# Hash-bucketed attention with a maxout layer behind it: one burst of eight heads in five chunks, 29 weight tiles, VectorE's third addition from the second batch on

## The chip, the cores and the metric

The kernel runs on one core of a Trainium2 chip. Its engines work side by side, each through its own list of instructions in order: TensorE (PE, matmuls; its weight loads are shown as PEld), VectorE (DVE), ScalarE (ACT), GpSimd (POOL) and SyncE (SP, which here only issues DMAs). They wait for each other by semaphores. SBUF is the memory on the chip that all engines work from, PSUM is what matmuls write into. The metric is the device time of one execution in microseconds, lower is better.

## The reference

Four batches, eight heads, 768 positions, 64 dimensions per head. Every query and key gets a bucket number of six bits, the signs of its six projections; a query attends only to keys of its own bucket. The heads' outputs side by side are the input of a layer whose hidden value is the largest of three products.

```python
q_bits = (np.einsum('bhsd,dk->bhsk', q, proj) > 0)        # the same for k
mask = q_bucket[:, :, :, None] == k_bucket[:, :, None, :]
scores = np.where(mask, scale * np.matmul(q, k.transpose(0, 1, 3, 2)), -1e9)
scores = scores - np.max(scores, axis=-1, keepdims=True)
attn = np.exp(scores)
attn = attn / (np.sum(attn, axis=-1, keepdims=True) + 1e-09)
x = np.matmul(attn, v)          # heads laid side by side: 3072 x 512
h = np.maximum(np.maximum(x @ w1, x @ w2), x @ w3)        # 3072 x 768
out = h @ w_out                                           # 3072 x 512
```

## The kernel before

**Chunks and units.** The queries of the first batch are cut into three chunks of 256 (chunks 0 to 2), those of each other batch into two of 384 (chunks 3 to 8). The bits are appended to queries and keys as further rows of the contraction, so that one matmul gives score and mask together. A *unit* is one matmul group of scores, 768 columns wide in all (for a 384-wide chunk: two key blocks of 128), and one exponential on ScalarE, which writes the unnormalised weights into one of `NAT = 24` weight tiles `AT` (`scores`, L298 and L306). A chunk of 384 has 24 units, three per head; there are 192 units, 48 per batch.

**The main loop** at the end of the kernel takes one step `u` per unit, and the order in which it issues instructions is the order on every engine: the scores of unit `u + 1`; whatever the lists `at` hold for this step; one feed-forward group (from the second batch on 1.15 per step, by a credit); a hash, if one is due; the bursts that are due (`todo`).

**A burst** (`burst`) turns the weights of four heads of a chunk into normalised attention. `sums` adds the weights over the keys by matmuls with a matrix of ones (L358), four heads side by side in four groups of 32 output columns. VectorE then transposes the sums (L365), adds a small number, takes the reciprocal and spreads it by a second transpose into `rb` (L369). `values` multiplies the weights with the value vectors, twice 24 matmuls (L380), and VectorE adds the sum of the values and multiplies with `rb` while it moves the result from PSUM into `xT` (L387). Then the weight tiles are free again. The burst of heads 0 to 3 of chunks 3 to 7 stands twelve steps ahead of that of heads 4 to 7, each four steps behind the last unit that it needs (`LAG`): steps 63 and 75 for chunk 3, 87 and 99 for chunk 4, 111 and 123 for chunk 5, 135 and 147 for chunk 6, 159 and 171 for chunk 7.

**Additions.** From chunk 3 on VectorE adds the three weight tiles of a head (`add`, L329, two instructions, each two steps behind its unit), so that the sums need two key blocks in place of six. From chunk `THIRD_ADD = 5` on a third, half as wide addition (L332) folds the two blocks into one.

**The feed-forward layer** of a chunk (`ffn_groups`) is put in line two steps behind its last burst and is worked off in the steps that follow, so that in steps 55 to 93 (units of chunks 3 and 4) the groups of the 256-wide chunks 1 and 2 are worked off. A group is four matmuls (L413) into one PSUM bank; of three groups the first is copied (by VectorE at L420 for 256-wide chunks, by ScalarE at L418 for 384-wide ones), the other two are taken into a running maximum by VectorE (L422). Final products (L457) come last in each chunk; ScalarE copies them out. Sums, values, hashes and groups share four PSUM banks, which are taken in the order in which they were given back (`bank`, `give`). The scores have two double banks of their own.

**Preparing heads.** From the second batch on queries and keys are loaded in sets of four heads (`load_quad`; sets 4 to 7 on GpSimd's queue), transposed by VectorE (`turn`, L202, four instructions a set and side), narrowed to bf16 by GpSimd (`narrow`, L207) and copied into place by DMAs on SyncE's queue (`place`). `quad_hash` makes the bits (L221, then one VectorE instruction, then four DMAs on SyncE's queue one step later) and is the last reader of the transposed tiles `t32`. `SPREAD` gives the steps of the transposes of sets 4 and 5 (from step 61) and 6 and 7 (from step 100).

Of the kernel before, what the change touches and what calls it, by code (L numbers as in the profile page):

```python
# [9 lines left out]
FP32 = mybir.dt.float32  # L10
FP16 = mybir.dt.float16
BF16 = mybir.dt.bfloat16
AluOp = mybir.AluOpType
# [4 lines left out]
def kernel(  # L18
# [12 lines left out]
    nc = tc.nc  # L31
    B, H, S, D = q.shape
    NBITS = proj.shape[1]
    P = 128
    NM = S // P
    HALF = S // 2
# [4 lines left out]
    Q = 32  # L41
# [8 lines left out]
    RS = 2.0 ** -5  # L50
    SCALE = 0.125 / (RS * RS)
    EPS = 2.0 ** -60
    NAT = 24
    SPREAD = {2: (61, 9), 3: (100, 12)}
    THIRD_ADD = 5
    LAG = (1, 4)
    ATW = 776

    konst = ctx.enter_context(tc.tile_pool(name="konst", bufs=1))
    nat_pool = ctx.enter_context(tc.tile_pool(name="nat", bufs=6))  # L60
    t32_pool = ctx.enter_context(tc.tile_pool(name="t32", bufs=3))
    t16_pool = ctx.enter_context(tc.tile_pool(name="t16", bufs=3))
    s_pool = ctx.enter_context(tc.tile_pool(name="spool", bufs=6))
    b_pool = ctx.enter_context(tc.tile_pool(name="bpool", bufs=2))
    vo_pool = ctx.enter_context(tc.tile_pool(name="vopool", bufs=4))
    small = ctx.enter_context(tc.tile_pool(name="small", bufs=4))
    ad_pool = ctx.enter_context(tc.tile_pool(name="adpool", bufs=5))
    ys_pool = ctx.enter_context(tc.tile_pool(name="yspool", bufs=2))
    rb_pool = ctx.enter_context(tc.tile_pool(name="rbpool", bufs=2))
    x_pool = ctx.enter_context(tc.tile_pool(name="xpool", bufs=3))  # L70
# [7 lines left out]
    pj2 = konst.tile([P, Q], FP32, name="pj2")  # L78
    pst = konst.tile([Q, 2, NBITS], FP32, name="pst")
    ones = konst.tile([P, Q], FP16, name="ones")  # L80
    at_tiles = [konst.tile([P, ATW], FP16, name=f"AT{i}", tag=f"AT{i}") for i in range(NAT)]
    warm = h_pool.tile([P, HALF], FP16, tag="ht", name="warm")
    w_sb = [konst.tile([P, NJC, DF], FP16, name=f"w{i}_sb", tag=f"w{i}_sb") for i in range(3)]
# [6 lines left out]
    def bank():  # L90
        i = free_banks.pop(0)
        return i, bank_tiles[i]

    def give(i):
        if i is not None:
            free_banks.append(i)


    nat, t32, t16, s_of, where, v_at = {}, {}, {}, {}, {}, {}
# [143 lines left out]
    def load_weights(i):  # L243
        if i == 3:
# [8 lines left out]
    chunks = [(b, w * n, w) for b in range(B) for w in (THIRD if b == 0 else HALF,)  # L253
              for n in range(S // w)]
    NCH = len(chunks)

    def parts_of(c):
        return chunks[c][2] * NM // (2 * HALF)
# [10 lines left out]

    at_free = list(range(NAT))  # L270
    at_form = [THIRD] * NAT
    at_of = {}
# [6 lines left out]
    def block_of(b, m):  # L279
        return 2 * (m % MH) + m // MH if b == 0 else m  # L280
# [29 lines left out]
    def weights_of(c, h, m):  # L310
        w = chunks[c][2]
        nb = 2 * HALF // w
        return blocks(at_tiles[at_of[unit_at[c, h, m // nb]]], w)[:, m % nb, :]
# [8 lines left out]
    def add(c, h, n):  # L322
# [6 lines left out]
        nc.vector.tensor_tensor(out=sum_of[c, h][:], in0=t[0], in1=t[n], op=AluOp.add)  # L329
        if n == 2 and c >= THIRD_ADD:  # L330
            t = sum_of[c, h]
            nc.vector.tensor_tensor(out=t[:, 0, :], in0=t[:, 0, :], in1=t[:, 1, :], op=AluOp.add)  # L332

    def sum_blocks(c, h):
        w = chunks[c][2]
        if (c, h) in sum_of:
            t = sum_of[c, h]
            return [t[:, j, 0:w] for j in range(1 if c >= THIRD_ADD else 2)]
        return [weights_of(c, h, m)[:, 0:w] for m in range(NM)]

    def burst(c, i):
        b, q0, w = chunks[c]
        held = {}
        rb = []

        def own_bank(key):
            if c == NCH - 1 and i == 1 and key != 1:
                return None, sc_ps.tile([P, 2, 512], FP32, tag="sc", name="sc")[:, 0, :]
            return bank()

        def sums(m0, m1):
            if m0 == 0:
                held["s"] = own_bank("s")
            sm = held["s"][1]
            bs = [sum_blocks(c, 4 * i + x) for x in range(4)]
            for m in range(len(bs[0])):
                for x in range(4):
                    nc.tensor.matmul(sm[Q * x : Q * (x + 1), 0:w], ones[:, :], bs[x][m],  # L358
                                     start=(m == 0), stop=(m == len(bs[0]) - 1))
            if m1 == NM:  # L360
                ys = ys_pool.tile([P, HALF], FP32, tag="ys", name="ys")
                rr = small.tile([P, HALF // Q], FP32, tag="rr", name="rr")
                n = w // Q
                rb.append(rb_pool.tile([P, HALF], FP32, tag="rb", name="rb"))
                nc.vector.transpose(ys[:, 0:w], sm[:, 0:w])  # L365
                give(held["s"][0])
                nc.vector.tensor_scalar(out=rr[:, 0:n], in0=ys[:, 0:w:Q], scalar1=EPS * S, scalar2=None, op0=AluOp.add)
                nc.vector.reciprocal(rr[:, 0:n], rr[:, 0:n])
                nc.vector.transpose(rb[0][:, 0:w], rr[:, 0:n].unsqueeze(2).to_broadcast((P, n, Q)))  # L369

        def values(side, m0, m1):
            if m0 == 0:
                held[side] = own_bank(side)
            av = held[side][1]
            first = (b, i, side) not in sv_of
            n = w + 1 if first else w
            for m in range(m0, m1):
                cb = block_of(b, m)
                for x in range(4):
                    nc.tensor.matmul(av[Q * x : Q * (x + 1), 0:n], v_at[2 * b + i][:, x, cb * D + side : (cb + 1) * D : 2],  # L380
                                     weights_of(c, 4 * i + x, m)[:, 0:n], start=(m == 0), stop=(m == NM - 1))
            if m1 == NM:
                if first:
                    sv_of[b, i, side] = small.tile([P, 1], FP32, tag=f"sv{side}", name="sv")
                    nc.vector.tensor_scalar(out=sv_of[b, i, side][:], in0=av[:, w : w + 1], scalar1=EPS, scalar2=None,
                                            op0=AluOp.mult)
                nc.vector.scalar_tensor_tensor(out=xt_of(c)[:, 2 * i + side, 0:w], in0=av[:, 0:w],  # L387
                                               scalar=sv_of[b, i, side][:], in1=rb[0][:, 0:w], op0=AluOp.add, op1=AluOp.mult)
                give(held[side][0])
                if side == 1:  # L390
                    for h in range(4 * i, 4 * i + 4):
                        for n in range(parts_of(c)):
                            a = at_of[unit_at[c, h, n]]
                            if b == 0 and i == 1:
                                nc.gpsimd.memset(blocks(at_tiles[a], HALF)[:, :, HALF : HALF + 2], 1.0)
                                at_form[a] = HALF
                            at_free.append(a)

        return sums, values


    def ffn_groups(c):
# [79 lines left out]
    with tc.manual_schedule():  # L482
# [10 lines left out]
        load_quad(1, 2, range(4), nc.sync)  # L493
        nc.vector.memset(pj2[:], 0.0)
        nc.vector.memset(ones[:], 1.0)
        for t in at_tiles:
            nc.vector.memset(blocks(t, THIRD)[:, :, THIRD : THIRD + 2], 1.0)
        for hd in range(2):
# [75 lines left out]
        hash_at = {}  # L574
        for g in range(2, NQUAD):
            b2, i2 = divmod(g, 2)
            need = UPB * b2 + 12 * i2
            for n, side in enumerate((1, 0)):
                name = (side, g)
                if g > 3:  # L580
                    us = [SPREAD[b2][0] + SPREAD[b2][1] * (8 * i2 + 4 * n + n2) // 4 for n2 in range(4)]
                    for x in range(4):
                        when(us[0] - 14 + x, load_quad, side, g, (x,), nc.gpsimd)
                else:
                    us = [need - {2: 26, 3: 23}[g] + 4 * n + n2 for n2 in range(4)]
                for n2, u2 in enumerate(us):
                    when(u2, turn, name, n2 // 2, n2 % 2)
                    if n2 % 2:
                        when(u2 + 1, narrow, name, n2 // 2)
                when(us[3] + 3, place, name, range(4))  # L590
            hash_at[{2: 32, 3: 47, 4: need - 12}.get(g, need - 9)] = g
            when({2: 36, 3: 46}.get(g, need - 22), load_v, g)

        ffn, credit = [], 0
        todo = {}
        last_of = {}
        for c, i in sorted(done_at, key=lambda e: done_at[e]):
            d = done_at[c, i] + LAG[c > 2]
            sums, values = burst(c, i)
            pieces = [lambda f=sums: f(0, NM), lambda f=values: f(0, 0, NM), lambda f=values: f(1, 0, NM)]  # L600
            for n, f in enumerate(pieces):
                u = {(0, 0): (16, 17, 20), (1, 0): (21, 22, 24), (2, 0): (26, 27, 29)}.get((c, i), (d, d, d))[n]
                todo.setdefault(u, []).append(f)
            last_of[c] = max(u, last_of.get(c, 0))
# [65 lines left out]
```

## Time and profile before

| | |
|---|---|
| median of three runs | 265.4 us (264.99 to 265.94) |
| the profiled execution | 265.08 us, its span 263.1 us |
| TensorE busy | 256.3 us (97%) |
| VectorE busy | 208.2 us (79%) |
| ScalarE busy | 177.7 us (68%) |
| GpSimd busy | 69.9 us (27%) |
| granted TensorE clock | 1.00 throughout |

A row of a timeline has the start in us, the duration in us, the engine, the line of the kernel, the operation, its output and input, their sizes, and the number of instructions that the row joins; square brackets hold idle time before it and what ended it. Durations of successive instructions overlap, since an engine starts one while the last ends: how long a row occupies its engine is read from its start to the start of the next. A row of the page's table of groups has the count, then busy time and the mean duration in ns, then idle time before. In a table of stretches each row is a stretch in us, with its length and the busy time of each engine.

### The profile page before, as it was taken

What the parts mean: (1) busy time and instruction counts of PE and PEld (TensorE: products, weight loads), DVE (VectorE), ACT (ScalarE), POOL (GpSimd) and SP (SyncE); (2) the same over time, 40 slices, a digit from 0 to 9 for tenths busy, and PEclk for the clock granted to TensorE, in tenths of its full rate; (3) what the DMA queues carried; (4) which work ended last, traced back from release to release, by engine and by line L of the source; (5) the groups of instructions that cost most, each with busy time, mean ns of one, the idle gap of its engine ahead of it and who ended that gap; (6) DMA issues with size and microseconds to landing.
All of it is one profiled execution on the core that took longest, in us unless ns stands there. A gap on an engine that the chain in (4) does not pass through costs nothing.

```text
span 263.1 us, 6479 instructions
## 1 busy us (share of the span) xinstructions
PE 256.3 (97%) x2503; PEld 154.1 (59%) x2503; DVE 208.2 (79%) x493; ACT 177.7 (68%) x257; POOL 69.9 (27%) x132
## 2 busy tenths in 40 slices
PE   7899999999999999999999999999999999999995
PEld 3555657866765666555555554555555555555552
DVE  2898767967799999969999996899949795888360
ACT  3697885667968675966869589484886859581322
POOL 2787752355043536230141612011000000000000
PEclk9999999999999999999999999999999999999999
DMA  6998899969732963970064662802030003000303
GB/s 194 328 232 163 169 241 232 217 115 206 199 88 67 196 154 51 274 193 18 0 182 120 103 138 46 212 0 60 17 122 1 0 2 121 2 0 2 120 0 120
DMA packets 20717, 30.95 MB, mean 118 GB/s; under 512 B 2608, under 2 KB 15248, under 8 KB 20688
## 3 DMA queue, kind: packets, MB, share of 16 engines
q0 software_dynamic: 8128, 13.37, 26.9%
q1 hardware_dynamic: 12128, 16.66, 22.0%
q10 hardware_dynamic: 432, 0.52, 0.6%
q8 instruction: 19, 0.31, 0.5%
q14 instruction: 10, 0.08, 0.1%
HBM read 25.17 MB, written 6.29 MB: 120 GB/s over the span
## 4 chain that ended last, share of the span: by engine, by line
PE 88%; DVE 5%; ACT 3%; issue 2%; POOL 1%; DVEq 0%; ACTq 0%
PE ms L413 33%; PE sc L298 22%; PE ms L457 11%; PE ms L380 11%; PE ms L221 3%; ACT AT L306 3%; PE ms L358 3%; PE ms L123 1%; PE ms L504 1%; PE ms L171 1%; DVE S L176 1%; DVE ht L422 1%; DVE ad L329 1%; PE ms L150 1%; POOL S L137 1%
## 5 line engine op out<-in xcount | busy, mean ns | idle before, releaser
L306 ACT ACTIVATE AT<-sc 128x768 f16<-128x768 f32 x192 | 152.7, 816 | 59.8 <-PE sc L298 56.1
L413 PE MATMUL ms<-xT,w_sb 128*128 128x384 f16 (+1 forms) x648 | 115.0, 307 | 0.3 <-DVE xT L387 0.2
L298 PE MATMUL sc<-S 72*128 72x384 bf16 (+1 forms) x432 | 93.8, 308 | 1.9 <-DVE S L176 0.8
L413 PEld LDWEIGHTS <-w_sb 128*128 128x128 f16 x648 | 62.7, 97 | 35.9 <-issue 0.4
L422 DVE TENSOR_TENSOR ht<-ht,ms 128x384 f16<-128x384 f16 (+1 forms) x108 | 54.2, 503 | 20.7 <-PE ms L413 10.4
L298 PEld LDWEIGHTS <-S 72*128 72x128 bf16 (+1 forms) x432 | 39.4, 98 | 33.0 <-issue 12.7
L207 POOL TENSOR_SCALAR T<-T 128x768 bf16<-128x768 f32 x24 | 22.9, 953 | 90.1 <-issue 48.4
L457 PE MATMUL ms<-wout_sb,ht 128*128 128x512 f16 x138 | 35.5, 378 | 0.0
L380 PE MATMUL ms<-AT,vo 128*32 128x385 f16 (+3 forms) x840 | 34.3, 308 | 0.0
L380 PEld LDWEIGHTS <-vo 128*32 128x32 f16 x864 | 22.9, 96 | 9.2 <-issue 1.7
L329 DVE TENSOR_TENSOR ad<-ad,AT 128x768 f16<-128x768 f16 x48 | 26.5, 553 | 2.1 <-ACT AT L306 1.3
L202 DVE STREAM_TRANSPOSE T<-nat 128x384 f32<-128x384 f32 x48 | 26.8, 564 | 0.0
L329 DVE TENSOR_TENSOR ad<-AT,AT 128x768 f16<-128x768 f16 x48 | 26.2, 546 | 0.2 <-ACT AT L306 0.2
L418 ACT CAST ht<-ms 128x384 f16<-128x384 f32 x36 | 17.3, 480 | 8.1 <-PE ms L413 8.1
L457 PEld LDWEIGHTS <-ht 128*128 128x128 f16 x138 | 13.3, 97 | 13.0 <-issue 0.3
L387 DVE SCALAR_TENSOR_TENSOR xT<-ms,sv,rb 128x384 f16<-128x384 f32 (+1 forms) x35 | 19.2, 565 | 1.3
L461 ACT COPY osb<-ms 128x512 f32<-128x512 f32 x21 | 12.3, 586 | 7.1 <-PE ms L457 5.8
L332 DVE TENSOR_TENSOR ad<-ad 128x384 f16<-128x384 f16 x32 | 15.5, 485 | 1.1
L137 POOL TENSOR_SCALAR S<-T 64x384 bf16<-64x384 f32 (+1 forms) x23 | 14.2, 617 | 5.0 <-DVE T L132 3.6
L196 POOL DMA_DIRECT2D nat<-in_q_dram x20 | 11.1, 560 | 0.1
L365 DVE STREAM_TRANSPOSE ys<-ms 128x384 f32<-128x384 f32 (+1 forms) x17 | 9.0, 531 | 2.3 <-PE ms L358 2.1
L176 DVE TENSOR_SCALAR S<-ms 6x384 bf16<-6x384 f32 x16 | 8.9, 554 | 2.0 <-PE ms L171 1.7
(52 smaller groups left out, 121.7 us busy)
## 6 DMA issues: line engine op xcount, KB each, us to landing
out_dram<-osb SPq DMA_DIRECT2D x21, 256.0 KB
S<-T SPq DMA_DIRECT2D x48, 96.0 KB
nat<-in_q_dram POOLq DMA_DIRECT2D x20, 192.0 KB, 6.1
vo<-in_v_dram POOLq DMA_DIRECT2D x8, 384.0 KB, 5.8
nat<-in_k_dram POOLq DMA_DIRECT2D x16, 192.0 KB, 5.7
w_sb<-in_moe_w_dram POOLq DMA_DIRECT2D x3, 768.0 KB, 10.4
nat<-in_k_dram SPq DMA_DIRECT2D x10, 192.0 KB
nat<-in_k_dram SPq DMA_DIRECT2D x3, 384.0 KB
```

What stands on the lines that cost most here:

```text
L137: nc.gpsimd.tensor_scalar(out=o, in0=i_, scalar1=RS, scalar2=1.0, op0=AluOp.mult, op1=AluOp.mult)
L202: nc.vector.transpose(t32[name][:, u, half * HALF : (half + 1) * HALF], i_)
L207: nc.gpsimd.tensor_scalar(out=t16[name][:, u, :], in0=t32[name][:, u, :], scalar1=RS, scalar2=1.0, op0=AluOp.mult, op1=AluOp.mult)
L298: nc.tensor.matmul(views[j], s_of[kn][0 : D + bits, kx, m * P : (m + 1) * P], s_of[qn][0 : D + bits, qx, q0 : q0 + w], start=True, stop=True)
L306: nc.scalar.activation(t[:, :, 0:w], whole, ActFn.Exp, bias=-SCALE * 0.25 * bits, scale=SCALE)
L329: nc.vector.tensor_tensor(out=sum_of[c, h][:], in0=t[0], in1=t[n], op=AluOp.add)
L380: nc.tensor.matmul(av[Q * x : Q * (x + 1), 0:n], v_at[2 * b + i][:, x, cb * D + side : (cb + 1) * D : 2], weights_of(c, 4 * i + x, m)[:, 0 ...
L387: nc.vector.scalar_tensor_tensor(out=xt_of(c)[:, 2 * i + side, 0:w], in0=av[:, 0:w], scalar=sv_of[b, i, side][:], in1=rb[0][:, 0:w], op0=A ...
L413: nc.tensor.matmul(ps[:, 0:w], w_sb[wi][:, jc, fb * P : (fb + 1) * P], xt[:, jc, 0:w], start=(jc == 0), stop=(jc == NJC - 1))
L418: nc.scalar.copy(hts[fb][:, 0:w], ps[:, 0:w])
L422: nc.vector.tensor_tensor(out=hts[fb][:, 0:w], in0=hts[fb][:, 0:w], in1=ps[:, 0:w], op=AluOp.max)
L457: nc.tensor.matmul(ps[:, 0:DM], hts[fb][:, tb * P : (tb + 1) * P], wout_sb[:, fb, :], start=(fb == 0), stop=(fb == NFB - 1))
```

## The change

- In chunks 3 to 7 one `burst_of_8` at the step of the second burst replaces both. Its sums are matmuls with `ones2`, a matrix of 32 columns for each of two halves: the first half of the heads is summed into 16 of the 32 output rows, the second into the other 16, in one PSUM bank. Transpose, addition and reciprocal are done once, with 24 numbers per partition in place of 12; the spreading transpose and the values remain two and four, as in two bursts.
- `THIRD_ADD` goes from 5 to 3: chunks 3 and 4 get the third addition too, 16 instructions in all, and their sums one key block in place of two.
- The weights of a whole chunk wait for the burst: 29 weight tiles (from 24) and 9 tiles of added weights (from 5). Room comes from the pools of loaded (6 to 5), transposed (3 to 2) and narrowed (3 to 2) heads.
- The transposes of sets 4 and 5 begin three steps earlier (58), and with them their loads; the hash of set 4 moves from step 84 to 75, that of set 6 from 135 to 123. The hashes of sets 5 and 7 stay at 99 and 147.
- The bursts of the first batch and of the last chunk remain, as does all else.

```diff
-    NAT = 24
-    SPREAD = {2: (61, 9), 3: (100, 12)}
-    THIRD_ADD = 5
+    NAT = 29
+    SPREAD = {2: (58, 9), 3: (100, 12)}
+    THIRD_ADD = 3
...
-    nat_pool = ctx.enter_context(tc.tile_pool(name="nat", bufs=6))
-    t32_pool = ctx.enter_context(tc.tile_pool(name="t32", bufs=3))
-    t16_pool = ctx.enter_context(tc.tile_pool(name="t16", bufs=3))
+    nat_pool = ctx.enter_context(tc.tile_pool(name="nat", bufs=5))
+    t32_pool = ctx.enter_context(tc.tile_pool(name="t32", bufs=2))
+    t16_pool = ctx.enter_context(tc.tile_pool(name="t16", bufs=2))
...
-    ad_pool = ctx.enter_context(tc.tile_pool(name="adpool", bufs=5))
+    ad_pool = ctx.enter_context(tc.tile_pool(name="adpool", bufs=9))
...
+    ones2 = konst.tile([P, 2, Q], FP16, name="ones2")
...
-        return sums, values
+        return sums, values, rb
+
+    def burst_of_8(c):
+        w = chunks[c][2]
+        n = w // Q
+        _, values0, rb0 = burst(c, 0)
+        _, values1, rb1 = burst(c, 1)
+        k_, sm = bank()
+        bs = [sum_blocks(c, h) for h in range(H)]
+        nb = len(bs[0])
+        for i in range(2):
+            for m in range(nb):
+                for x in range(4):
+                    nc.tensor.matmul(sm[Q * x : Q * (x + 1), 0:w], ones2[:, i, :], bs[4 * i + x][m],
+                                     start=(i == 0 and m == 0), stop=(i == 1 and m == nb - 1))
+        ys = ys_pool.tile([P, HALF], FP32, tag="ys", name="ys")
+        rr = small.tile([P, n, 2], FP32, tag="rr2", name="rr2")
+        rr1 = rr.rearrange("p n i -> p (n i)")
+        nc.vector.transpose(ys[:, 0:w], sm[:, 0:w])
+        give(k_)
+        nc.vector.tensor_scalar(out=rr1, in0=ys[:, 0 : w : Q // 2], scalar1=EPS * S, scalar2=None, op0=AluOp.add)
+        nc.vector.reciprocal(rr1, rr1)
+
+        def spread(i, rb):
+            rb.append(rb_pool.tile([P, HALF], FP32, tag="rb", name="rb"))
+            nc.vector.transpose(rb[0][:, 0:w], rr[:, :, i : i + 1].to_broadcast((P, n, Q)))
+
+        spread(0, rb0)
+        values0(0, 0, NM)
+        spread(1, rb1)
+        values0(1, 0, NM)
+        values1(0, 0, NM)
+        values1(1, 0, NM)
...
+        nc.vector.memset(ones2[:], 0.0)
+        for i in range(2):
+            nc.vector.memset(ones2[:, i, i * Q // 2 : (i + 1) * Q // 2], 1.0)
...
-            hash_at[{2: 32, 3: 47, 4: need - 12}.get(g, need - 9)] = g
+            hash_at[{2: 32, 3: 47, 4: 75, 5: 99, 6: 123, 7: 147}[g]] = g
...
-            sums, values = burst(c, i)
+            if 2 < c < NCH - 1:
+                if i == 1:
+                    todo.setdefault(d, []).append(lambda c=c: burst_of_8(c))
+                    last_of[c] = d
+                continue
+            sums, values, _ = burst(c, i)
```

## The prediction

> **What bounds the kernel now.** I read the page first, then the waits, then TensorE's and VectorE's timelines side by side around the bursts.
>
> ```profile
> span 263.1 us, 6479 instructions
> PE 256.3 (97%) x2503; PEld 154.1 (59%) x2503; DVE 208.2 (79%) x493; ACT 177.7 (68%) x257; POOL 69.9 (27%) x132
> 73.39:87.11 13.72, 13.58 (x134) 8.69 (x132) 13.34 (x33) 10.33 (x15) 6.27 (x9) 1.00 0.36 100
> 87.11:100.78 13.67, 13.67 (x150) 9.02 (x148) 13.39 (x35) 9.32 (x13) 4.59 (x7) 1.00 0.67 143
> 117.08:132.52 15.44, 15.44 (x137) 8.91 (x129) 14.64 (x31) 10.26 (x15) 2.19 (x3) 1.00 0.10 26
> ```
>
> TensorE is busy for 97% of the span, so the time is its work plus its gaps. The last three lines are stretches from one burst to the next, twelve steps each (columns: length, then busy time of PE, weight loads, DVE, ACT, POOL, then clock, DMA share, GB/s). In the first two VectorE is busy for 13.34 of 13.72 us and 13.39 of 13.67: the average of 79% hides a stage in which it has nothing left. These are the steps of the second batch whose feed-forward groups belong to the 256-wide chunks of the first batch.
>
> How close VectorE is there to holding TensorE up is seen in one place. TensorE's rows, then VectorE's:
>
> ```profile
> 76.67 0.49 PE L298 MATMUL sc<-S 72*128 72x384 bf16 x2
> 77.00 0.60 PE L413 MATMUL ms<-xT,w_sb 128*128 128x256 f16 x4
> 77.43 0.49 PE L298 MATMUL sc<-S 72*128 72x384 bf16 x2
> ...
> 78.53 0.60 PE L413 MATMUL ms<-xT,w_sb 128*128 128x256 f16 x4
> ...
> 80.93 0.49 PE L298 MATMUL sc<-S 72*128 72x384 bf16 x2
> 81.57 0.60 PE L413 MATMUL ms<-xT,w_sb 128*128 128x256 f16 x4
> ...
> 81.10 0.93 DVE L422 TENSOR_TENSOR ht<-ht,ms 128x256 f16<-128x256 f16 x2
> ```
>
> The start of one row to the start of the next is what an instruction group occupies: scores 0.33 us (76.67 to 77.00), a group 0.43, a step 0.76. At 80.93 the scores take 0.64 until the next start: a gap of 0.31. The group at 81.57 uses the PSUM bank of the fourth group before it, the one at 78.53, whose maximum VectorE begins only at 81.10, two microseconds after that group's matmuls ended (78.53 + 0.60 = 79.13). So **the cover is about 2.0 us**: with four banks, VectorE may be that late, and what it is late beyond this TensorE waits. It is all that TensorE lost in these two stretches (13.58 of 13.72, 13.67 of 13.67 busy, the rest rounding), but it means that there is no reserve left at this point.
>
> **The change part by part.**
>
> *Sums and bursts on TensorE (a gain).*
>
> ```profile
> 146.28 0.81 PE L413 MATMUL ms<-xT,w_sb 128*128 128x384 f16 x4
> 146.93 0.49 PE L298 MATMUL sc<-S 72*128 72x384 bf16 x2
> 147.26 0.81 PE L413 MATMUL ms<-xT,w_sb 128*128 128x384 f16 x4
> 148.00 0.35 PE L358 MATMUL ms<-ad,ones 128*32 128x384 f16 x4
> 148.18 2.14 PE L380 MATMUL ms<-AT,vo 128*32 128x385 f16 x48
> 150.25 0.50 PE L298 MATMUL sc<-S 72*128 72x384 bf16 x2
> ...
> 97.04 1.50 PE L221 MATMUL ms<-T,pj 128*32 128x384 f32 x16
> 98.47 0.50 PE L298 MATMUL sc<-S 72*128 72x384 bf16 x2
> ...
> 115.76 1.50 PE L221 MATMUL ms<-T,pj 128*32 128x384 f32 x16
> 117.08 0.51 PE L358 MATMUL ms<-ad,ones 128*32 128x384 f16 x8
> 117.40 2.13 PE L380 MATMUL ms<-AT,vo 128*32 128x384 f16 x48
> ```
>
> A group of 384 columns occupies 0.65 us before scores (146.28 to 146.93) and 0.74 before a burst (147.26 to 148.00): going into the 32-column form costs 0.09. A hash followed by scores takes 1.43 (97.04 to 98.47), followed by sums 1.32 (115.76 to 117.08): coming out costs 0.11. Each separate visit to that form thus costs 0.20. Six visits go: the bursts of heads 0 to 3 in the five chunks, and the hash of set 4, which stood alone at step 84 and now sits directly before the burst at step 75. (The hash of set 6 moves from one burst, step 135, to another, 123: its visit went with that burst.) 6 x 0.20 = 1.2 us. Sums: in chunks 3 and 4 each burst of four heads takes 8 matmuls, 0.32 (117.08 to 117.40); the burst of eight takes 8 for all eight heads, so 2 x 0.33 = 0.67 us go. In chunks 5 to 7 two times 4 matmuls (0.18 each, 148.00 to 148.18) become 8: nothing. The value matmuls are the same. **Gain on TensorE: 1.9 us**, all on the path.
>
> *The work after the sums on VectorE (a gain, mostly hidden).*
>
> ```profile
> 74.81 0.57 DVE L365 STREAM_TRANSPOSE ys<-ms 128x384 f32<-128x384 f32 x1
> ...
> 75.88 0.58 DVE L369 STREAM_TRANSPOSE rb<-rr 128x384 f32<-128x384 f32 x1
> ...
> 77.79 0.55 DVE L329 TENSOR_TENSOR ad<-ad,AT 128x768 f16<-128x768 f16 x1
> ```
>
> A burst of four occupies VectorE for 2.98 us (74.81 to 77.79), of which transpose, addition and reciprocal are 1.07 (to 75.88). One of these threes goes per chunk. In chunks 5 to 7 VectorE isn't the bound (14.64 of 15.44 us with a burst in it; without one 14.64 - 2.98 = 11.7 of some 13), so it is worth nothing there. The burst of eight is one block: 2 x 2.98 - 1.07 = 4.9 us on VectorE after the sums, beside 2 x 2.07 = 4.1 us of values on TensorE (148.18 to 150.25 is 2.07). Its five PSUM banks are one more than there are: the last values take that of the sums, which the transpose frees 0.6 us into the 4.1, so TensorE doesn't wait. But VectorE leaves it 0.8 us late, where two separate bursts gave two chances to catch up.
>
> *The third addition in chunks 3 and 4 (a loss on VectorE).*
>
> ```profile
> L332 DVE TENSOR_TENSOR ad<-ad 128x384 f16<-128x384 f16 x32 | 15.5, 485 | 1.1
> ...
> 121.12 0.52 DVE L329 TENSOR_TENSOR ad<-ad,AT 128x768 f16<-128x768 f16 x1
> 121.67 0.36 DVE L332 TENSOR_TENSOR ad<-ad 128x384 f16<-128x384 f16 x1
> 121.94 0.55 DVE L422 TENSOR_TENSOR ht<-ht,ms 128x384 f16<-128x384 f16 x1
> ...
> 131.64 0.86 DVE L332 TENSOR_TENSOR ad<-ad 128x384 f16<-128x384 f16 x1
> ...
> 131.25 1.05 POOL L207 TENSOR_SCALAR T<-T 128x768 bf16<-128x768 f32 x1 [5.55 <-DVE T L202]
> ...
> 70.42 0.55 DVE L329 TENSOR_TENSOR ad<-AT,AT 128x768 f16<-128x768 f16 x1
> 70.89 0.41 DVE L422 TENSOR_TENSOR ht<-ht,ms 128x256 f16<-128x256 f16 x1
> 71.22 0.57 DVE L202 STREAM_TRANSPOSE T<-nat 128x384 f32<-128x384 f32 x1
> 71.72 0.52 DVE L329 TENSOR_TENSOR ad<-ad,AT 128x768 f16<-128x768 f16 x1
> ```
>
> Undisturbed it occupies 0.27 (121.67 to 121.94), and lengthens the addition in front of it from about 0.45 to 0.55 (121.12 to 121.67), 0.38 in all. Beside a narrowing on GpSimd (131.25 to 132.30) it lasts 0.86 in place of 0.36. All 32 have a mean of 485 ns, 0.13 above 0.36. I take 0.38 + 0.10 = **0.48 us** each, since the eight narrowings of sets 4 and 5 fall into the same stretch; the ends are 0.38 (never beside GpSimd) and 0.98 (always).
>
> A rule bears on this. The Trainium skill, "GPSIMD Engine Reference", Specifications, says that GpSimd shares its SBUF interfaces with VectorE and contends with VectorE instructions that are in a two-port mode or have two SBUF inputs; the rows at 131.25 and 131.64 agree. Its page "VectorE: DVE Perf Modes", under why tensor_tensor can't do the higher modes, says that such an addition never takes a two-port mode, and read alone that would let the third addition pass at 0.38: the forecast would fall by the 0.8 us that the low end gives among the rivals. The measured 0.86 decides against reading it alone.
>
> *Where these meet: steps 58 to 70 and 76 to 89.* Per step VectorE does: additions (0.47 + 0.45)/3 = 0.30; transposes of the loaded heads (71.22 to 71.72 is 0.50), 16 in 34 steps, 0.24; 1.15 maxima or copies at 0.33 (70.89 to 71.22), 0.38; together 0.92. TensorE's step is 0.33 + 1.15 x 0.435 = 0.83. VectorE so loses 0.09 us a step already, and 0.5 us at each burst (2.98 beside 0.32 + 2.07); it gains this back where the groups are final products, whose copies ScalarE makes, and at hashes. With the third addition, 0.48/3 = 0.16, VectorE's step is 1.08 and it loses 0.25.
> First stretch: the transposes now begin at 58 (before 61), and up to step 70 there are 13 steps with neither a burst nor a final product: 13 x 0.25 = 3.3 us late, less the cover of 2.0: TensorE waits 1.3. Then four final products (steps 71 to 74) and the hash bring VectorE back.
> Second stretch: after the burst of eight, 0.8 late, 14 steps (76 to 89; the burst at 87 and the hash at 84 are gone from it): 0.8 + 14 x 0.25 = 4.3, less 2.0: 2.3.
> New waits 3.6 us; the 0.31 of before is in them. Steps in the third and fourth batch last longer on TensorE (0.33 + 1.15 x 0.65 = 1.08 us), VectorE's additions with the third are there already, and the cover isn't used up: zero.
>
> *The tiles and pools.* Twenty-nine weight tiles are what a whole chunk (24) and five steps of lag need: the list runs empty right at each burst of eight, and the next exponential waits on scores that stand behind that burst anyway. Five tiles are no longer set on GpSimd, since they aren't used by heads 4 to 7 of the first batch: VectorE sets their last columns before scores 48 to 52.
>
> ```profile
> 60.76 1.58 ACT L306 ACTIVATE AT<-sc 128x768 f16<-128x768 f32 x2 [2.15 <-POOL AT L395]
> ```
>
> An exponential does wait for such a setting (2.15 us here, on GpSimd). Some 60 ns each, but in VectorE's queue behind a burst: between 0 and 0.5 us, I take 0.2. One natural, one transposed and one narrowed buffer less: each is freed ten steps or more before it is taken, but for the transposed ones, which the hash of the set before frees one step earlier, hence the moved hashes; on TensorE they precede the burst of 4 us, so the next transposition finds them done. Loads for set 4 are issued three steps earlier on GpSimd's queue, the moved hashes send their bits (four DMAs on SyncE's queue each) 9 and 12 steps earlier, ahead of copies that are due in the same step: no one waits for them that soon. Nothing for these. The added settings at the start lie in VectorE's wait for the projection.
>
> *Sum.* 265.08 (profiled execution, 263.1 span and 2.0 around it) - 1.9 - 0.3 + 3.6 + 0.2 = 266.7; the median shown, 265.4, is 0.3 above that execution: **267.0 us**.
>
> **The rivals.**
> *Faster: VectorE's lateness stays under cover.* If the third addition passes at 0.38, a loss of 0.22 a step, the new waits are 13 x 0.22 - 2.0 = 0.9 and 0.8 + 14 x 0.22 - 2.0 = 1.9, 2.8 in all, and the time 265.4 - 1.9 - 0.3 + 2.8 + 0.2 = 266.2; with a cover of 3 us as well, 0.0 and 0.9, and 264.3; with no wait at all 263.4. It decides from new waits under about 1.2 us on. For it: VectorE, busy 97%, now causes a gap of only 0.31. Against: that gap appeared at a lateness of 2.0.
> *No change:* new waits between 1.2 and 2.8 us: 264.6 to 266.2.
> *Slower by more: every third addition meets GpSimd.* At 0.98 each VectorE loses 0.42 a step: 13 x 0.42 - 2.0 = 3.5, 0.8 + 14 x 0.42 - 2.0 = 4.7, 8.2 together, 271.6. For it: narrowings of 1 us and additions follow the same transposes. Against: 0.13 above the undisturbed on average.
> *ScalarE becomes the bound,* since it starves through 4.5 us of burst and then needs 24 exponentials.
>
> ```profile
> 66.73 5.32 ACT L306 ACTIVATE AT<-sc 128x768 f16<-128x768 f32 x7
> ```
>
> Back to back they take (5.32 - 0.81)/6 = 0.75 each; 24 of them and two output copies, 19 us, against 24 x 0.83 = 20: it just keeps pace, and if it loses 1 us in chunks 3 and 4 the time is 269. Little speaks for it.
>
> **How the numbers follow.** Forecast, waits of 2.8 to 5.2 us, 266.2 to 268.6: 0.42. More than that, by GpSimd: 0.19; by ScalarE: 0.05. No change, within 0.3% (0.8 us, about what a measurement of this kernel can tell): 0.14. Faster: 0.20, at 263.4 to 264.6. So slower 0.66. The range, 263.9 to 270.0, leaves out the best of the faster case and the end of the GpSimd case; for the likeliest case alone it is 266.2 to 268.6.
>
> **What would show it.** TensorE's waits on VectorE's maxima (or starts of its rows further apart than 0.76) between about 68 and 72, and again between 90 and 103 us; VectorE above 97% busy from 70 to 100 us; no wait of TensorE from 120 us on, and there each chunk shorter by 0.2. Third additions of 0.86 beside narrowings. One sums row of 8 matmuls per chunk, 96 value matmuls behind it. Wrong it would be if VectorE's lateness passes 2 us without a gap on TensorE, if the burst of eight itself stalls on its banks, or if the visits to the 32-column form cost less than 0.2.

## The result, and the profile after

The changed kernel takes 273.38 us (median, 271.83 to 274.61) where the kernel before takes 265.33 us: 3.1% slower, ratio 1.0307 with a 95% interval of 1.0273 to 1.0340. The forecast was 267.0 us, its range ended at 270.0: the sign was right, the size far off. Its four executions fall into two pairs, 271.8 and 272.3 us, and 274.5 and 274.6; the profile is of the second pair, and the last section comes back to them.

The first lines of the page after, then the two stretches in question (from the first transpose of set 4 to the burst of chunk 3, from there to that of chunk 4; columns as before), then TensorE's waits by cause (total us, times, longest). Lines of the kernel after stand one to 34 higher: L447 is the group of the feed-forward layer (L413 before), L456 its maximum (L422), L299 the scores (L298), L307 the exponential.

```profile
span 272.7 us, 6445 instructions
PE 258.6 (95%) x2487; PEld 156.2 (57%) x2487; DVE 212.1 (78%) x507; ACT 177.2 (65%) x257; POOL 69.8 (26%) x132
```
```profile
70.02:89.76 19.74, 17.52 (x130) 11.18 (x131) 19.12 (x44) 15.17 (x21) 9.24 (x13) 1.00 0.43 113
89.76:121.45 31.69, 28.82 (x276) 18.15 (x272) 28.84 (x67) 20.82 (x29) 9.37 (x14) 1.00 0.67 140
```
```profile
PE sc L299 <- ACT AT L307: 3.0, 4, 1.9
PE ms L447 <- DVE ht L456: 2.3, 3, 1.1
PE ms L447 <- DVE ht L454: 1.8, 2, 1.0
```

TensorE now idles in chunks 3 and 4 (17.52 busy of 19.74, 28.82 of 31.69; before it lost 0.3 us there), and VectorE is what it waits for. Beside that there is a cause that the forecast's sum doesn't have at all: scores that wait for an exponential.

TensorE's timeline, first stretch and second; where two starts lie further apart than the work between them, there is a wait.

```profile
77.82 0.49 PE L299 MATMUL sc<-S 72*128 72x384 bf16 x2
79.36 1.12 PE L447 MATMUL ms<-xT,w_sb 128*128 128x256 f16 x8 [1.05 <-DVE ht L456]
...
103.17 0.49 PE L299 MATMUL sc<-S 72*128 72x384 bf16 x2
104.66 0.60 PE L447 MATMUL ms<-xT,w_sb 128*128 128x256 f16 x4 [1.00 <-DVE ht L454]
```

From 77.82 to 79.36 are 1.54 us for scores of 0.33: 1.21 lost. Counted this way over all rows, the first stretch loses 2.9 us and the second 3.8. The other loss stands at the end of chunk 3's feed-forward layer; ScalarE's rows, then TensorE's:

```profile
139.16 0.58 ACT L495 COPY osb<-ms 128x512 f32<-128x512 f32 x1
...
141.05 0.58 ACT L495 COPY osb<-ms 128x512 f32<-128x512 f32 x1
...
144.67 0.58 ACT L495 COPY osb<-ms 128x512 f32<-128x512 f32 x1 [2.32 <-DMA out_dram<-osb]
```
```profile
143.73 0.81 PE L447 MATMUL ms<-xT,w_sb 128*128 128x384 f16 x4
146.40 0.48 PE L299 MATMUL sc<-S 72*128 72x384 bf16 x2 [1.86 <-ACT AT L307]
146.72 1.14 PE L447 MATMUL ms<-xT,w_sb 128*128 128x384 f16 x4
147.66 0.85 PE L299 MATMUL sc<-S 72*128 72x384 bf16 x2
148.29 1.49 PE L447 MATMUL ms<-xT,w_sb 128*128 128x384 f16 x4
149.57 0.85 PE L299 MATMUL sc<-S 72*128 72x384 bf16 x2
```

The third output row waits 2.3 us for a buffer that the first row's DMA still reads (there are two); the exponentials stand behind it in ScalarE's queue and the scores behind those: 2.0 us. Then TensorE runs at half its rate: a group takes 1.28 us (148.29 to 149.57) in place of 0.65, until about 150; 1.7 us more. The span of the profiled execution is 9.6 us longer than that of before (272.7 for 263.1). Of these the parts above make 8.8: 2.9 + 3.8 - 0.3 (the wait that was there) in chunks 3 and 4, 2.0 + 1.7 here, and 0.6 for the settings of the five tiles, less the 1.9 gained. Some 0.5 more lies at the start: the first scores come at 8.46 in place of 7.70, and chunk 3's first at 55.39 in place of 54.91. I don't count it as the change's: the next kernel has the same start and its first scores at 7.72, and in the other profiled executions, of either start, they lie anywhere between 7.2 and 8.3. The rest, 0.3, is left over.

### The profile page after: what moved, and what is told of

Same layout as the page of the kernel before. It is cut to its first block, busy times and chain, and to the rows that moved or that the text cites. A ratio compares the mean times of both kernels' runs of the same rounds, so it can differ in the third digit from the quotient of the medians.

```text
span 272.7 us, 6445 instructions
## 1 busy us (share of the span) xinstructions
PE 258.6 (95%) x2487; PEld 156.2 (57%) x2487; DVE 212.1 (78%) x507; ACT 177.2 (65%) x257; POOL 69.8 (26%) x132
## 4 chain that ended last, share of the span: by engine, by line
PE 49%; DVE 10%; DMA 4%; issue 2%; ACT 1%; DVEq 0%; ACTq 0%
PE ms L447 23%; PE sc L299 10%; PE ms L491 7%; PE ms L381 5%; DVE ad L330 3%; DVE ht L456 2%; DMA nat<-in_q_dram 2%; DMA out_dram<-osb 2%; PE ms L222 2%; DVE T L203 2%; DVE ad L333 1%; DVE ht L454 1%; PE ms L472 0%; DVE xT L388 0%; ACT osb L495 0%
## 5 line engine op out<-in xcount | busy, mean ns | idle before, releaser
L307 ACT ACTIVATE AT<-sc 128x768 f16<-128x768 f32 x192 | 152.1, 816 | 66.4 <-PE sc L299 63.6
L447 PE MATMUL ms<-xT,w_sb 128*128 128x384 f16 (+1 forms) x648 | 116.5, 310 | 4.5 <-DVE ht L456 2.3
L299 PE MATMUL sc<-S 72*128 72x384 bf16 (+1 forms) x432 | 94.4, 310 | 4.2 <-ACT AT L307 3.0
L447 PEld LDWEIGHTS <-w_sb 128*128 128x128 f16 x648 | 63.1, 97 | 41.9 <-issue 6.7
L456 DVE TENSOR_TENSOR ht<-ht,ms 128x384 f16<-128x384 f16 (+1 forms) x108 | 54.3, 504 | 28.1 <-PE ms L447 14.9
L299 PEld LDWEIGHTS <-S 72*128 72x128 bf16 (+1 forms) x432 | 40.1, 98 | 34.2 <-issue 13.5
L381 PE MATMUL ms<-AT,vo 128*32 128x385 f16 (+3 forms) x840 | 33.4, 308 | 0.0
L381 PEld LDWEIGHTS <-vo 128*32 128x32 f16 x864 | 23.6, 96 | 8.4 <-issue 1.3
L333 DVE TENSOR_TENSOR ad<-ad 128x384 f16<-128x384 f16 x48 | 23.2, 484 | 1.6
L454 DVE CAST ht<-ms 128x256 f16<-128x256 f32 x18 | 7.4, 411 | 2.6 <-PE ms L447 2.6
```

Source lines behind the costliest of these rows:

```text
L299: nc.tensor.matmul(views[j], s_of[kn][0 : D + bits, kx, m * P : (m + 1) * P], s_of[qn][0 : D + bits, qx, q0 : q0 + w], start=True, stop=True)
L307: nc.scalar.activation(t[:, :, 0:w], whole, ActFn.Exp, bias=-SCALE * 0.25 * bits, scale=SCALE)
L447: nc.tensor.matmul(ps[:, 0:w], w_sb[wi][:, jc, fb * P : (fb + 1) * P], xt[:, jc, 0:w], start=(jc == 0), stop=(jc == NJC - 1))
L456: nc.vector.tensor_tensor(out=hts[fb][:, 0:w], in0=hts[fb][:, 0:w], in1=ps[:, 0:w], op=AluOp.max)
```

## The experiments

All of them are set against the kernel before on the same chip, at a median of 264.9 to 265.0 us. The changed kernel was measured beside a median of 265.3, so that a difference between an experiment and its 273.38 us is uncertain by some 0.4 us.

**Three output rows.** One more buffer, and one less of the transposed sums for room.

```diff
-    ys_pool = ctx.enter_context(tc.tile_pool(name="yspool", bufs=2))
+    ys_pool = ctx.enter_context(tc.tile_pool(name="yspool", bufs=1))
-    o_pool = ctx.enter_context(tc.tile_pool(name="opool", bufs=2))
+    o_pool = ctx.enter_context(tc.tile_pool(name="opool", bufs=3))
```

> Edit: the changed kernel with three buffers for output rows (two before) and, for room, one for the transposed sums (two before). Theory A (the two output-row buffers: without the burst at step 111 the three final products of chunk 3 stand closer together, the third copy waits for the first row's DMA, ScalarE waits 2.3 us, TensorE 2.0, and TensorE then runs some 3 us at half its rate, 1.7 us more): the wait at the end of chunk 3 goes, granted clock 1.00, 2.0 to 3.7 us faster than the changed kernel, about 270.5. Rival B (the DMAs on SyncE's queue are late there whatever the buffers): a wait of about 2 us stays in that place, 273. The waits in chunks 3 and 4 (6.7 us) stay by both.

270.17 us, ratio 1.0195 (1.0180 to 1.0210), 3.2 us faster than the change. ScalarE's timeline in the same place:

```profile
138.41 0.58 ACT L495 COPY osb<-ms 128x512 f32<-128x512 f32 x1
...
141.53 0.60 ACT L495 COPY osb<-ms 128x512 f32<-128x512 f32 x1
```

The third copy waits no more, and TensorE runs at full rate behind it: theory A. Before the change the burst at step 111 stood between the products of the first row and the third (132.61 to 134.86) and kept the third copy behind the DMA; the burst of eight took it away. The third experiment, where that burst is back and the buffers are two, has no such wait either. The waits of chunks 3 and 4 are the same within 0.02 us each.

**Third addition from chunk 5 on.**

```diff
-    THIRD_ADD = 3
+    THIRD_ADD = 5
```

> Edit: the changed kernel with the third addition from chunk 5 on, as before the change; its bursts of eight sum two key blocks in chunks 3 and 4. Theory V (VectorE has more work than TensorE in the steps of chunks 3 and 4 between bursts; sixteen additions of some 0.55 us are most of it): waits there fall from 6.7 to about 1 us, TensorE has 0.7 us more of sums, in all 5 us faster than the changed kernel, about 268.5, with the output-row wait still there. Rival R (the burst of eight itself costs the time, as a block of 4.4 us during which VectorE falls behind): waits stay at 5 us or more, 272 to 274.

267.64 us, ratio 1.0105 (1.0075 to 1.0135): 5.7 faster. Waits in chunks 3 and 4 fall from 6.7 to 1.9 us, with the burst of eight in place. Theory V, though it had put the rest at 1 and the time at 268.5.

**Bursts of four, all else as changed.**

```diff
-            if 2 < c < NCH - 1:
+            if False:
                 if i == 1:
```

> Edit: the changed kernel with two bursts of four in chunks 3 to 7 as before; 29 tiles, third addition from chunk 3, smaller pools and moved hashes stay. Theory V: VectorE's surplus of 0.28 us a step stays, but each stretch is broken by a burst in which TensorE spends 2.5 us and VectorE 3.0; waits in chunks 3 and 4 fall from 6.7 to about 4.6; the output-row wait goes with the burst back between the final products (3.7 us); 1.0 us of visits to the 32-column form returns. About 269 to 270. Rival R (the burst of eight is what costs): the waits of chunks 3 and 4 go, 265.5 to 266.5.

271.87 us, ratio 1.0269 (1.0250 to 1.0288). Rival R falls: without the burst of eight the kernel is hardly faster, though this form has no output-row wait, and it is 1.7 us slower than the burst of eight with three output rows. But the 269 to 270 of theory V is missed too: counted from start to start, chunks 3 and 4 and the sums in them lose some 7 us here, where 4.6 were expected, so that a burst in the middle of a stretch is no relief. VectorE's lateness now also meets TensorE at the sums. The same is seen in the next kernel.

**The third addition alone, in the kernel before.**

```diff
-    THIRD_ADD = 5
+    THIRD_ADD = 3
```

> Edit: the kernel before with the third addition from chunk 3 on, and nothing else of the change. Theory V (the third addition is the loss, whatever the bursts): VectorE gets 16 x 0.55 = 8.8 us more in a stage that had no reserve, TensorE 0.7 us less; waits in chunks 3 and 4 rise from 0.3 to 5 or 6 us; about 269.5. Rival P (the waits come from the earlier transposes, the moved hashes and the smaller pools): no more than 266.

270.46 us, ratio 1.0209 (1.0194 to 1.0224), 1 us above what was expected. One number of the change costs 5.5 us, against the 8 of the whole, in a kernel without any other part of it. TensorE's timeline at the burst of chunk 4's heads 0 to 3:

```profile
104.46 0.34 PE L358 MATMUL ms<-ad,ones 128*32 128x384 f16 x3
105.70 0.32 PE L358 MATMUL ms<-ad,ones 128*32 128x384 f16 x1 [0.90 <-DVE ad L332]
```

The fourth head's sum waits for its third addition: 1.24 us from start to start for the three matmuls in front of it, where all four take 0.17 without a wait (89.08 to 89.25).

**Tiles, pools, transposes and hashes alone,** in the changed kernel.

```diff
-    THIRD_ADD = 3
+    THIRD_ADD = 5
...
-            if 2 < c < NCH - 1:
+            if False:
                 if i == 1:
```

> Edit: the changed kernel with bursts of four and the third addition from chunk 5 on: what is left of the change is the 29 tiles, the smaller pools, the earlier transposes and the moved hashes. Theory V: 0.6 us for the settings of five tiles on VectorE ahead of the first exponentials of chunk 3, 0.2 saved for the hash of set 4 that no longer stands alone, waits of chunks 3 and 4 about as before: 265.2 to 265.8. Rival P: 268 or more, with waits in chunks 3 and 4.

268.42 us, ratio 1.0128 (1.0114 to 1.0142): a miss, 3.5 us for what I had put at 0.2 to 0.8, and the time that rival P gave. The next kernel divides it.

**Transposes and hashes alone, in the kernel before.**

```diff
-    SPREAD = {2: (61, 9), 3: (100, 12)}
+    SPREAD = {2: (58, 9), 3: (100, 12)}
...
-            hash_at[{2: 32, 3: 47, 4: need - 12}.get(g, need - 9)] = g
+            hash_at[{2: 32, 3: 47, 4: 75, 5: 99, 6: 123, 7: 147}[g]] = g
```

> Edit: the kernel before with the transposes of sets 4 and 5 from step 58 and the hashes of sets 4 and 6 at steps 75 and 123, and nothing else of the change. Theory H (the hash at step 84 stood in the middle of the second stretch and gave VectorE 1.4 us in which to catch up; at step 75 it stands before a burst, and the transposes come three steps earlier into a stage that is full): 2 to 2.5 us slower than before, 267.2, with waits in chunks 3 and 4 and at the sums. Rival Q (the 3.5 us of the sixth experiment come from the smaller pools and the 29 tiles): within 0.5 us of before.

267.56 us, ratio 1.0096 (1.0075 to 1.0117): theory H. TensorE's timeline:

```profile
81.97 0.49 PE L298 MATMUL sc<-S 72*128 72x384 bf16 x2
82.79 0.60 PE L413 MATMUL ms<-xT,w_sb 128*128 128x256 f16 x4 [0.33 <-DVE ht L422]
...
102.38 0.34 PE L358 MATMUL ms<-ad,ones 128*32 128x384 f16 x3
103.31 0.49 PE L358 MATMUL ms<-ad,ones 128*32 128x384 f16 x5 [0.58 <-DVE ad L329]
```

No instruction is added, and yet VectorE holds TensorE up in both stretches. Counted from start to start, TensorE loses some 0.9 us in the first (0.3 before). These waits, near 80 to 83 us, stand ahead of the hash in both kernels (88.51 here, 97.04 before), so they come with the earlier transposes. Some 1.6 us lie in the second stretch, the sums behind it and the first steps after them. There theory H fits: the hash that stood in its middle, with 1.4 us of TensorE work and only 0.5 of VectorE's behind it, was a rest for VectorE. But the transposes moved in the same run, and the two weren't tried apart. The remaining 0.9 us of the sixth experiment (268.42 less 267.56) belong to the tiles and pools, 0.6 of it by TensorE's wait at the first exponentials of chunk 3.

**Copies on ScalarE for chunks 1 and 2,** in the changed kernel.

```diff
-                    if w == HALF:
+                    if w == HALF or c in (1, 2):
                         nc.scalar.copy(hts[fb][:, 0:w], ps[:, 0:w])
```

> Edit: the changed kernel, but the copy that begins each group of three in the feed-forward layer is made by ScalarE for chunks 1 and 2 too (by VectorE before, 0.33 us each). Theory V: eleven such copies leave VectorE in the two stretches, 3.6 us less of its work there, and the waits of 6.7 us fall by about that: 270 us. Rival S (ScalarE, with 0.75 us of exponential and now 0.13 of copy in a step of 0.83, becomes the bound): half of that or less, 272 us and TensorE waiting on exponentials.

269.36 us, ratio 1.0147 (1.0090 to 1.0204): 4.0 faster, the waits of chunks 3 and 4 down from 6.7 to about 2.9. ScalarE has room: its timeline there shows 0.37 for a copy and no wait behind it.

```profile
70.58 0.37 ACT L452 CAST ht<-ms 128x256 f16<-128x256 f32 x1
70.83 2.27 ACT L307 ACTIVATE AT<-sc 128x768 f16<-128x768 f32 x3
```

So VectorE's work is what counts, whether the third additions go or other work does.

**The burst of eight without its waits:** third addition from chunk 5, three output rows, and the five tiles set by GpSimd.

```diff
-                            if b == 0 and i == 1:
+                            if b == 0 and (i == 1 or a in (11, 20, 21, 22, 23)):
                                 nc.gpsimd.memset(blocks(at_tiles[a], HALF)[:, :, HALF : HALF + 2], 1.0)
```

> Edit: the changed kernel with the third addition from chunk 5 on, three output-row buffers (one for the transposed sums), and the last columns of the five tiles set by GpSimd when heads 0 to 3 of the first batch leave them. Theory V and A together: against the kernel of the second experiment the output-row wait (2.6 us) and the 0.6 us at step 49 go, 1.9 us of waits in chunks 3 and 4 remain against 1.2 saved on visits to the 32-column form: 265.0 to 265.6, the kernel before within 0.3%. If the burst of eight has a cost of its own that I haven't seen, 266.5 or more.

264.76 us, ratio 0.9989 (0.9979 to 1.0000): level with before. 1.7 us of waits in chunks 3 and 4 are left to eat the gain.

**And the copies on ScalarE,** on top of that.

```diff
-                    if w == HALF:
+                    if w == HALF or c in (1, 2):
```

> Edit: as the kernel before this one, and the copies that begin each group of three are made by ScalarE for chunks 1 and 2 too. Theory V: VectorE's step in those stretches falls from 0.92 to about 0.80 us, below TensorE's 0.83, and the remaining waits of 1.9 us go almost all, so that the saved visits are seen: 263.5 to 264.2, faster than the kernel before by 0.3% to 0.5%. Rival S (ScalarE is the bound in that stage now): 265 or more, TensorE waiting on exponentials.

263.53 us, ratio 0.9946 (0.9934 to 0.9959): faster than both kernels. The two stretches of this kernel, up to the hash before each burst of eight:

```profile
66.00:84.50 18.50, 18.44 (x134) 12.77 (x132) 15.33 (x33) 18.04 (x31) 9.31 (x13) 1.00 0.57 149
84.50:112.20 27.70, 27.70 (x278) 18.07 (x277) 23.65 (x53) 21.10 (x34) 9.32 (x14) 1.00 0.71 154
```

VectorE is busy for 15.33 of 18.50 and 23.65 of 27.70 us, and TensorE all the time. ScalarE is near its own end in the first (18.04 of 18.50), without holding TensorE up.

Two controls say whose gain that is. The same edit in the kernel before, alone:

> Edit: the kernel before with the copies that begin each group of three made by ScalarE for chunks 1 and 2. Theory V: TensorE waited only 0.31 us there, so no more than 0.3 us are gained: 264.6 to 264.9. If more is gained, the gain of the eighth experiment is not the burst's.

265.30 us, ratio 1.0008 (0.9995 to 1.0020): nothing, or too little to see. And the fastest kernel with bursts of four in place of eight:

```diff
-            if 2 < c < NCH - 1:
+            if False:
                 if i == 1:
```

> Edit: the kernel of the eighth experiment with two bursts of four in chunks 3 to 7 in place of one of eight. If the burst of eight is worth its five visits to the 32-column form (5 x 0.20 = 1.0 us) and the third of VectorE's work that it saves, and has no cost where VectorE has reserve: 264.5 to 265, 1.0 to 1.5 us slower than the eighth. If the gain of the eighth came from the copies alone: 263.5.

264.82 us, ratio 0.9992 (0.9982 to 1.0003). The burst of eight alone is worth 1.3 us where VectorE has reserve.

## Why the prediction was wrong, by its steps

**Put together by medians:** 265.0 before; transposes and hashes + 2.6 (267.56); tiles and pools + 0.9 (268.42); third addition + 3.4 (271.87); burst of eight + 1.5 (273.38), which is - 1.7 for itself and + 3.2 for the output rows. Each is what it adds on top of those named ahead of it; alone, the third addition costs 5.5. The sum is 8.4 where the change itself measured 8.05 (273.38 less 265.33): the last step compares medians that were taken beside different ones of before.

**The gain on TensorE was right.** Five visits were put at 1.0 us, and the burst of eight was worth 1.3 in the controls and 1.7 in the changed kernel; what VectorE's smaller work adds to that wasn't divided. The rows of the changed kernel, TensorE's and VectorE's at the burst of chunk 3:

```profile
88.45 1.50 PE L222 MATMUL ms<-T,pj 128*32 128x384 f32 x16
89.76 0.51 PE L414 MATMUL ms<-ad,ones 128*32 128x384 f16 x8
90.09 4.13 PE L381 MATMUL ms<-AT,vo 128*32 128x385 f16 x96
94.15 0.50 PE L299 MATMUL sc<-S 72*128 72x384 bf16 x2
...
90.07 0.56 DVE L225 TENSOR_SCALAR bits<-ms 128x384 bf16<-128x384 f32 x1 [0.29 <-issue]
90.55 0.57 DVE L419 STREAM_TRANSPOSE ys<-ms 128x384 f32<-128x384 f32 x1
...
95.52 0.57 DVE L203 STREAM_TRANSPOSE T<-nat 128x384 f32<-128x384 f32 x1
```

Hash 1.31, sums 0.33, values 4.06 without a break: the banks suffice, as forecast. VectorE's part takes 4.97 (90.55 to 95.52; forecast 4.9).

**The third addition's price was right, the step made of it was not.** All 48 third additions have a mean of 484 ns; the 32 of before had 485. What failed is "VectorE's step is 1.08 and it loses 0.25". It is an average over 34 steps with undisturbed durations. The group's row, then VectorE's rows of the first seven steps, 58 to 64:

```profile
L333 DVE TENSOR_TENSOR ad<-ad 128x384 f16<-128x384 f16 x48 | 23.2, 484 | 1.6
...
70.02 0.57 DVE L203 STREAM_TRANSPOSE T<-nat 128x384 f32<-128x384 f32 x1
...
71.06 0.36 DVE L333 TENSOR_TENSOR ad<-ad 128x384 f16<-128x384 f16 x1
71.34 0.42 DVE L454 CAST ht<-ms 128x256 f16<-128x256 f32 x1
71.86 0.42 DVE L456 TENSOR_TENSOR ht<-ht,ms 128x256 f16<-128x256 f16 x1
...
73.46 0.85 DVE L330 TENSOR_TENSOR ad<-ad,AT 128x768 f16<-128x768 f16 x1
...
74.62 0.42 DVE L454 CAST ht<-ms 128x256 f16<-128x256 f32 x1
...
78.11 0.86 DVE L333 TENSOR_TENSOR ad<-ad 128x384 f16<-128x384 f16 x1
78.90 0.93 DVE L456 TENSOR_TENSOR ht<-ht,ms 128x256 f16<-128x256 f16 x2
```

From 70.02 to 78.90 are 8.9 us for seven steps, 1.27 a step, so that VectorE loses 0.44 against TensorE's 0.83. Three things add to the average: both narrowings meet an addition (0.85 and 0.86; I had counted on the third ones alone, but the second, with two tiles read, is held up just so); a copy with the maximum that reads it right behind occupies 0.52 from start to start (71.34 to 71.86), not 0.33, twice; and transposes and third additions stand closer in these steps than on average. The lateness of 2.0 us at which TensorE begins to wait held: TensorE's first wait of the first stretch, 0.30 us behind the scores of 74.46, is for a bank whose group ended at about 72.65 and which VectorE began to read at 74.62.

**The lateness after a burst of eight** was put at 0.8 us and is 1.4 (94.15 to 95.52). The hash was moved directly ahead of it, and its bits (0.48, 90.07 to 90.55) stand in VectorE's queue before the sums. I had counted the moved hash as rest for VectorE at the end of the first stretch, and not this end of it.

**"Nothing for these", of the moved work, was wrong.** By the forecast's own sum, transposes and hashes without the third addition leave 13 x 0.09 - 2.0 and 0.8 + 14 x 0.09 - 2.0, no waits at all; the ninth experiment measured 2.6 us. I take it for the same step that failed: an average step of 0.92 hides that VectorE was already at its end where the items stand thick.

**The output rows are missing from the prediction.** It said of the third and fourth batch that the cover isn't used up: true of VectorE, but TensorE lost 3.2 us there by ScalarE, and the sign "no wait of TensorE from 120 us on" failed. The step that failed is the list of what the early bursts did: they cost TensorE 0.2 us each and VectorE a third of its work, but they also kept two final products apart. The trace of before gave a hint of it, in the burst's rows and that of the first row's DMA:

```profile
132.61 0.35 PE L358 MATMUL ms<-ad,ones 128*32 128x384 f16 x4
...
134.86 0.50 PE L298 MATMUL sc<-S 72*128 72x384 bf16 x2
...
133.44 0.34 SPq L463 DMA_DIRECT2D out_dram<-osb  x1
```

The DMA was issued at 133.44, and ScalarE copied into its buffer again at 138.25, 4.8 us later, of which the burst made 2.25. After the change the same DMA, issued at 139.76, freed the buffer only at 144.67, 4.9 us later.

**The settings of the five tiles:** 0.6 us, where 0.2 was taken and 0.5 the upper end.

**The rivals.** GpSimd in the way of the additions happened at about every narrowing, yet a third addition cost what the forecast took. That this rival's 271.6 us comes nearest to the measured time is luck: it needs every third addition at 0.98 us, and 0.98 is a slip besides, since 0.38 and the 0.50 of a narrowing make 0.88. ScalarE was not the bound by its amount of work; TensorE did wait for exponentials, but because of an output buffer.

## What to carry to other kernels

In a stage whose second engine is 97% busy, price a change by that engine's rows in the steps where they stand thickest, with their waits on each other, and not by an average step; there, moving work costs time too, 2.6 us here. Before a block of work is taken out of a stream, list what else it kept apart: buffers with two turns, queues and DMAs that were just in time. And when a saving on the bounding engine is lost to another, look for work to take off that other one: here six copies per chunk on an engine with room turned 264.8 into 263.5 us.

## What the runs showed of the hardware that I had not expected

**TensorE at half its rate after a short wait.** After 1.86 us without work the matmuls of the changed kernel took 0.32 us per 384 columns for some 3 us (148.29 to 149.57 for four); stretches from the end of the wait show a granted clock of 0.59, then 0.96.

```profile
146.40:150.20 3.80, 3.80 (x14) 1.86 (x14) 2.55 (x6) 2.65 (x4) 0.00 (x0) 0.59 0.13 48
150.20:154.00 3.80, 3.80 (x24) 2.26 (x23) 3.01 (x7) 2.71 (x4) 1.14 (x2) 0.96 0.02 4
```

It doesn't always come: two of the four executions were at a clock of 0.994 (274.5 and 274.6 us) and two at 0.998 to 1.000 (271.8 and 272.3). With the copies on ScalarE in the changed kernel, a wait of 2.30 us was followed by half rate again (1.28 us for a group, from 144.54); in the second experiment one of 2.40 us was followed by full rate at once:

```profile
142.00 0.48 PE L299 MATMUL sc<-S 72*128 72x384 bf16 x2 [2.40 <-ACT AT L307]
142.32 0.81 PE L447 MATMUL ms<-xT,w_sb 128*128 128x384 f16 x4
142.97 0.49 PE L299 MATMUL sc<-S 72*128 72x384 bf16 x2
```

So a wait of 2.0 us costs 2.0 or, with the half rate behind it, 3.7. The Trainium skill, "TensorE: Matmul & The Clock Gate", Part 1, tells of a gate that halves the clock after an idle window of about 3.4 us, and of windows that run freely, whatever the kernel does; the halving agrees, and that it hits one execution and not the next would fit free windows, but here 1.86 us were enough, about half a window. Why they are enough wasn't tried.

**An addition with two tiles as inputs waits for GpSimd.** In the changed kernel the second addition takes 0.52 to 0.56 alone and 0.85 where it begins during a narrowing, the third 0.36 and 0.86 (78.11, with a narrowing from 77.73 to 78.77). The maxima, which read one tile and PSUM, keep their 0.41. From chunk 3 on nearly every narrowing of the changed kernel meets one of the two additions.
